# A long convolution with an MLP: three of K's channel blocks transposed by DMA, table G built from its non-zero parts

## The chip, the core and the metric

The kernel runs on one NeuronCore of a Trainium2 chip. The core has TensorE (PE, matmuls; PEld is its weight load), VectorE (DVE), ScalarE (ACT), GpSimd (POOL) and SyncE (SP), which here only issues transfers. Each engine works through its own list in order; they wait for each other by semaphores. SBUF is the on-chip memory of 128 partitions, PSUM the eight banks that TensorE writes and that ACT or DVE must empty ("evict") into SBUF. Sixteen DMA engines move data for all queues.

The metric is the device time of one execution in microseconds (us). The median of three runs before the change is 221.71 us (221.61 to 222.79).

## What is computed

```python
def reference(A_q, A_k, A_v, A_shift_k, A_ssm_k, A_ssm_D, B_x, B_w1, B_b1, B_w2):
    def _A_ref(q, k, v, shift_k, ssm_k, ssm_D):
        ...
        k_pad = jnp.pad(k, ((0, 0), (ks - 1, 0), (0, 0)))
        for t in range(ks):
            k_shift = k_shift + k_pad[:, t:t + S, :] * shift_k[:, ks - 1 - t][None, None, :]
        kv = k_shift * v
        ...
        y_f = kv_f * kf_f[None, :, :, :]
        y = irfft2(y_f)[:, 0, :S, :]
        y = y + kv * ssm_D[None, None, :]
        return q * y
    ...
    x = A_q
    h = x + _A_ref(_layernorm(x, axis=-1), A_k, A_v, A_shift_k, A_ssm_k, A_ssm_D)
    h2 = h + _B_ref(_layernorm(h, axis=-1), B_w1, B_b1, B_w2)
    return h2
```

(The two FFT calls are shortened in this listing.) There are 2048 positions and 640 channels, all bf16; the shift filter has four taps, the long filter ssm_k has 2048, and the MLP `_B_ref` is 640 to 1728 to 640 with the activation h * tanh(softplus(h)).

## The kernel before

**The algorithm.** The long causal convolution is a Fourier transform written as matmuls. The 640 channels are five blocks of 128 (dc, b or m = 0 to 4), grouped in three chunks: blocks 0 and 1, blocks 2 and 3, block 4. A transform has two stages: stage 1 (s1) is a matmul with cosine and sine tables over 128 positions, stage 2 (s2) one small matmul for each of 128 frequencies with a 128 x 128 matrix from table G. This is done for the filter (k in names: s1k, s2k) and for the product kv (v in names: s1v, s2v). Then the two spectra are multiplied (p1, p2; for p2 the filter's spectrum is needed with its partitions swapped in pairs, which the DMAs sw provide), and an inverse in two stages (i1, i2) gives y. Layernorms, the gate by q, and the MLP in two matmuls (m1, m2) follow.

**From raw K to kv.** K is loaded with positions on the partitions, in four parts (d_k0 to d_k3, line 525) into `ra`. For each block and each half h of a row's 16 positions, 8 transposes on TensorE (ktpe, line 590) bring the channels onto the partitions; the result, 1024 bf16 columns in one PSUM bank, is evicted by ACT or DVE (ktev, line 593, by the helper at lines 426 to 430) into `kt_s`. A third copy, shifted by one column, is made by GpSimd (ktsh, line 601). The shift filter is then a matmul (kspe, lines 609 and 610) with small banded matrices `wsh`, built by GpSimd (line 516); the eviction multiplies by V (kv, line 613, DVE).

**Table G.** It is a 128 x 16384 table (4 MB) that holds, for each frequency, a 128 x 128 matrix which is block-diagonal over four interleaved channels, so three quarters of it are zeros. It is loaded in eight pieces (d_g0 to d_g7, line 541), each as far as possible with long rows, and read as weights with step 1 (`g_v`, line 366) at lines 662 (s2k, 128 matmuls of 160 columns) and 697 (s2v, 128 of 64 and 128 of 96 columns).

**The order.** Every piece of work is an operation with a name, a cost and its dependencies; the list ORDER (lines 26 to 97) says in which order they go and, after the colon, on which engine: t TensorE, a ACT, v DVE, p GpSimd, d SP's DMA queue, s ACT's DMA queue. `_schedule` (line 181) walks the list and sets a start time for each from its cost and dependencies, and the operations are emitted by these times. So each engine's own order is that of the list. The names of the halves end in x and y. In the list before, SP's order is: the filter's five blocks d_n, x0, all of K, then pieces of G and the two halves of V (d_v1 early, d_v0 after four pieces of G), then the swaps sw0_1, sw0_0, sw2_0, sw0_3, sw0_2, sw1_0, d_a12, sw1_1, sw2_1, then the inverse's table and the weights of the MLP. GpSimd builds wsh, makes the shifted copies and takes nine of the sixteen products p1/p2 of chunk 0.

Of the kernel before, what the change touches and what calls it, by code (L numbers as in the profile page):

```python
# [12 lines left out]
BF16 = mybir.dt.bfloat16  # L13
# [3 lines left out]
S = 2048  # L17
D = 640
FF = 1728
FP = 1792  # L20
P = 128
# [5 lines left out]
d_id:s wz:v d_dr:s d_sk:s d_go:d wm:t d_n0:d d_n2:d d_n3:d d_x0:d d_n1:d d_n4:d d_k2:d dcpe:t warm:a dcev:v dq0:v k1pe0y:t k1pe0x:t k1pe2y:t d_k3:d  # L27
k1ev0y:v d_k1:d dq2:v k1pe2x:t k1ev0x:v k1ev2y:v k1ev2x:a s1kpe0_0x:t s1kev0_0x:v d_k0:d s1kpe0_3x:t s1kpe0_1y:t s1kpe0_2x:t s1kpe0_2y:t s1kpe2_2x:t
s1kpe2_3x:t s1kpe2_0y:t s1kev0_3x:a ln1_2:v s1kev0_2y:a s1kev0_2x:a dq1:v cfpe:t kz:p ln1p2:p s1kev2_3x:a dq3:v s1kev2_2x:a ln1_3:v s1kev0_1y:v dq4:v
d_g4:d k1pe3y:t k1ev3y:a coef:a d_v1:d wsh4_0:p ln1p3:p k1pe1x:t d_g3:d d_g2:d k1ev1x:a wsh2_1:p wsh0_0:p wsh4_1:p wsh1_1:p wsh3_1:p wsh2_0:p d_g1:d  # L30
k1pe1y:t k1pe3x:t k1ev1y:v k1pe4y:t k1pe4x:t k1ev3x:v k1ev4x:v s1kpe1_0y:t s1kpe2_2y:t s1kpe1_1y:t wsh1_0:p s1kev2_2y:a s1kpe2_1y:t k1ev4y:v
s1kpe3_0x:t s1kev1_0y:a s1kev2_0y:a s1kpe2_1x:t s1kpe1_1x:t s1kpe0_3y:t s1kev0_3y:a s1kev3_0x:v s1kev1_1x:v s1kpe4_0x:t s1kev4_0x:v s1kpe4_3y:t
s1kev4_3y:a s1kpe4_3x:t s1kpe2_0x:t s1kev2_1x:a s1kpe3_2y:t s1kpe4_2x:t ln1_0:v s1kev4_3x:v s1kev3_2y:v s1kev2_1y:a s1kpe0_1x:t s1kpe2_3y:t
s1kev1_1y:v ktpe2y:t s1kev4_2x:a ktev2y:v ktpe1y:t ktpe3y:t ktpe4y:t ktpe0x:t ktpe4x:t ktev1y:a ln1_1:v d_v0:d ktpe0y:t ktev3y:a s1kev2_0x:v ktev4x:v
ktev4y:v s1kev2_3y:a s1kev0_1x:a ktev0y:a ktpe3x:t ktpe2x:t s1kpe3_3y:t s1kpe3_2x:t s1kev3_3y:v s1kpe4_0y:t s1kpe4_1y:t s1kpe4_1x:t s1kev4_1y:a
s1kev3_2x:a s1kpe3_3x:t s1kpe1_3y:t ktev0x:v s1kpe0_0y:t ktev3x:v kspe3_1y:t s1kpe1_0x:t ktev2x:a s1kev1_3y:a s1kev4_0y:a ktpe1x:t s1kpe3_1y:t d_g0:d
s1kev1_0x:a s1kev0_0y:a s1kev3_1y:a s1kpe3_1x:t ktsh4:p wsh0_1:p s1kev4_1x:v ktsh1:p wsh3_0:p ktsh2:p ktsh0:p ln1p1:p ktsh3:p s1kev3_3x:v kv3_1y:v
s1kpe4_2y:t s1kpe1_2y:t ktev1x:v s1kev4_2y:a s1kev3_1x:v s1kpe1_2x:t d_small:p s1kpe3_0y:t s1kev1_2y:v s1kpe1_3x:t kspe0_1x:t kspe1_1x:t s1kev3_0y:v
s1kev1_2x:a s1kev1_3x:a s2kpe_9y:t s2kev_9y:a s2kpe_6x:t s2kev_6x:a s2kpe_5x:t s2kpe_3x:t s2kpe_10y:t kv0_1x:v s2kev_10y:a kv1_1x:v s2kpe_7y:t d_g6:d
d_g7:d d_g5:d s2kev_5x:v s2kpe_10x:t s2kev_3x:a kspe0_1y:t s2kpe_3y:t s2kev_3y:a s2kev_7y:v s2kpe_4x:t kspe0_0x:t s2kpe_6y:t kv0_1y:v kv0_0x:v  # L40
kspe0_0y:t s2kev_4x:a s2kev_6y:a kspe1_0x:t s2kpe_4y:t s2kev_10x:a kv0_0y:v s2kpe_8y:t s2kpe_7x:t s2kpe_8x:t s2kpe_2x:t kspe1_0y:t s2kev_4y:a
s2kpe_9x:t s2kev_7x:a kv1_0x:v s2kev_8x:a kspe1_1y:t s2kpe_5y:t s2kev_8y:v s1vpe0_2x:t kv1_0y:v s1vpe0_1x:t kv1_1y:v s1vev0_1x:v s1vpe0_1y:t
s1vpe0_0y:t s2kev_9x:a ln1p0:p s1vpe1_0x:t s1vpe1_0y:t s1vev0_0y:v s2kev_2x:a s2kev_5y:a s1vev0_2x:v s1vev0_1y:a s1vpe0_0x:t s1vpe1_2x:t s1vpe1_3y:t
s1vev1_3y:v s1vev1_2x:v s1vev1_0y:a s1vpe0_3x:t s1vpe1_2y:t s1vev1_0x:a s1vpe1_1x:t s1vev1_1x:v s1vpe0_2y:t s1vpe1_3x:t s1vev0_0x:v s1vev0_3x:a
s1vpe0_3y:t s1vpe1_1y:t s1vev1_2y:a s2kpe_15y:t kspe2_1x:t s1vev0_2y:a s1vev1_3x:a s1vev0_3y:a kv2_1x:v s2kpe_1x:t s2kpe_1y:t kspe4_0x:t kspe3_1x:t
s2kpe_20y:t s1vev1_1y:a s2vpe0_0x:t s2kev_1x:a s2kpe_0y:t kspe3_0x:t kv4_0x:v kv3_1x:v s2kev_1y:a kspe3_0y:t s2vpe0_4x:t s2kev_0y:a s2kev_20y:a
s2vpe0_3x:t s2vpe0_3y:t s2vev0_4x:a s2vev0_0x:v kv3_0y:v s2kev_15y:v s2vev0_3y:a kspe2_0y:t s2kpe_20x:t s2vev0_3x:a s2kpe_2y:t kspe4_1y:t s2vpe0_2x:t
s2kev_20x:a s2kev_2y:a kv3_0x:v s2kpe_17y:t s2kpe_14x:t s2vpe0_0y:t sw0_1:d s2vpe0_2y:t kv2_0y:v s2vev0_2x:v s2vev0_0y:v s2kev_17y:a s2kev_14x:a
kspe4_0y:t s2kpe_0x:t kspe2_1y:t s1vpe3_0x:t s2vev0_2y:a s2kev_0x:a kv4_0y:v kv4_1y:v s1vpe3_0y:t s1vev3_0y:a s2kpe_18x:t kspe2_0x:t s2kpe_19x:t
s2kpe_21:t p2_0_3:p p1_0_3:p s2kev_18x:a s1vev3_0x:a s2vpe0_6x:t kv2_0x:v s2kpe_16y:t s2kev_16y:a s2kpe_14y:t s2vpe0_1x:t s2vev0_1x:a s2kev_21:v  # L50
# [945 lines left out]
```

## Time and profile before

| what | us |
|---|---|
| median of three runs (lowest, highest) | 221.71 (221.61, 222.79) |
| profiled execution: span, first to last instruction | 219.6 |
| the same execution's whole time | not listed; runs' median less span: 2.1 |
| TensorE busy | 212.6 |
| weight loads busy | 157.8 |
| DVE busy | 145.1 |
| ACT busy | 133.1 |
| GpSimd busy | 75.6 |

The granted TensorE clock was 1.000 throughout. The page has six parts: busy time by engine; the span in 40 slices of about 5.5 us, each digit the busy share in tenths; the DMA queues; the chain of work that ended last; the costliest groups of instructions; and the DMA issues. In a group's row, `out<-in` are the names of tiles, then follow partitions x elements, the count, busy time, mean length of one in ns, and after the second bar the idle time of the engine just before, with what ended it. Busy time of TensorE includes the latency of a pipelined matmul, so two matmuls that overlap have lengths above their distance. The distance of two starts is what counts for throughput: in the rows of a timeline, that is the length of a group less the length of one, divided by the count less one.

### The profile page before, as it was taken

The numbers are of one execution on the slowest core, as the hardware profiler recorded it, in microseconds if no ns is written. First come the engines' busy times: TensorE is split into PE (matmuls) and PEld (weight loads), VectorE is DVE, ScalarE is ACT, GpSimd is POOL, SyncE is SP. The second block draws the span as 40 slices with busy tenths as digits, with TensorE's granted clock in tenths as the row PEclk, the third lists the DMA queues.
The fourth block names the chain that finished last, engine by engine and source line by source line (L and its number), as shares of the span: only waits on it lengthen the run. The fifth ranks groups of instructions, "written<-read, shape, count | busy, mean of one in ns | idle before, by whom it ended". The sixth has DMA issues, their size and how long they took to land.

```text
span 219.6 us, 6285 instructions
## 1 busy us (share of the span) xinstructions
PE 212.6 (97%) x2611; PEld 157.8 (72%) x2618; DVE 145.1 (66%) x324; ACT 133.1 (61%) x265; POOL 75.6 (34%) x112
## 2 busy tenths in 40 slices
PE   8999999999989999999999999999999999999993
PEld 2899889999879999899876644566554444656672
DVE  0799999999999999989699889883210000213023
ACT  2488899999999999997881178600036475300000
POOL 0079997089844007124883371411000000000000
PEclk9999999999999999999999999999999999999999
DMA  6999993417999906996004401552720000000113
GB/s 213 375 419 414 412 403 130 98 23 174 192 263 285 380 10 217 325 359 105 0 0 64 91 14 45 50 103 60 86 79 19 0 3 0 0 0 3 54 60 125
DMA packets 32876, 31.03 MB, mean 141 GB/s; under 512 B 19024, under 2 KB 29264, under 8 KB 32464
## 3 DMA queue, kind: packets, MB, share of 16 engines
q1 hardware_dynamic: 32384, 30.43, 46.3%
q8 instruction: 20, 0.33, 0.7%
q10 hardware_dynamic: 368, 0.20, 0.4%
q14 instruction: 8, 0.07, 0.1%
q0 software_dynamic: 96, 0.00, 0.0%
HBM read 20.47 MB, written 2.62 MB: 105 GB/s over the span
## 4 chain that ended last, share of the span: by engine, by line
PE 76%; ACT 11%; DVE 5%; issue 3%; SPq 2%; DMA 1%; DVEq 0%; ACTq 0%
PE ps L943 26%; PE ps L910 26%; ACT uk L428 8%; PE ps L813 4%; ACT uv L428 3%; PE ps L756 3%; PE ps L757 3%; PE ps L635 2%; PE ps L561 2%; PE ps L473 2%; PE ps L590 2%; DMA xa<-uk 1%; DVE ra L613 1%; PE ps L931 1%; DVE uv L716 1%
## 5 line engine op out<-in xcount | busy, mean ns | idle before, releaser
L910 PE MATMUL ps<-G 128*128 128x512 bf16 (+1 forms) x319 | 58.5, 336 | 0.3
L943 PE MATMUL ps<-rn,uv 128*128 128x320 bf16 (+2 forms) x415 | 58.5, 299 | 0.1
L915 ACT ACTIVATE uv<-ps,b1s 128x512 bf16<-128x512 f32 (+1 forms) x65 | 35.6, 607 | 36.6 <-PE ps L910 34.8
L943 PEld LDWEIGHTS <-uv 128*128 128x128 bf16 x416 | 39.2, 98 | 18.5 <-issue 1.6
L910 PEld LDWEIGHTS <-G 128*128 128x128 bf16 x325 | 31.1, 98 | 24.0 <-issue 0.9
L428 ACT CAST uk<-ps 128x512 bf16<-128x512 f32 (+1 forms) x91 | 47.2, 703 | 1.9 <-PE ps L562 1.4
L948 DVE TENSOR_TENSOR xb<-ps,xb 128x320 bf16<-128x320 f32 (+2 forms) x12 | 5.6, 488 | 42.6 <-ACT uv L915 24.3
L428 ACT CAST uv<-ps 128x512 bf16<-128x512 f32 (+2 forms) x54 | 28.6, 766 | 0.0
L430 DVE CAST uk<-ps 128x512 bf16<-128x512 f32 (+2 forms) x32 | 20.1, 661 | 0.6 <-ACT uk L428 0.5
L756 PE MATMUL ps<-a,uv 128*128 128x128 bf16 x160 | 18.7, 219 | 0.4 <-DVE uv L716 0.3
L756 PEld LDWEIGHTS <-uv 128*128 128x128 bf16 x160 | 17.8, 114 | 0.9 <-DVE uv L716 0.5
L837 POOL TENSOR_TENSOR r<-ve,mhalf 128x1 f32<-128x1 f32 x16 | 9.7, 613 | 25.0 <-DVE ve L834 24.9
L430 DVE CAST uv<-ps 128x512 bf16<-128x512 f32 (+2 forms) x28 | 17.2, 669 | 0.2 <-ACT uv L428 0.2
L948 DVE TENSOR_TENSOR xa<-ps,xa 128x320 bf16<-128x320 f32 x12 | 5.6, 486 | 14.0 <-PE ps L943 13.9
L613 DVE TENSOR_TENSOR ra<-ps,rb 128x512 bf16<-128x512 f32 x20 | 12.9, 683 | 0.3 <-ACT uv L428 0.3
L720 POOL TENSOR_TENSOR rn<-rn,uv 128x1024 bf16<-128x1024 bf16 x5 | 10.6, 2127 | 7.2 <-PE ps L697 7.2
L697 PE MATMUL ps<-uv,G 128*128 128x64 bf16 (+1 forms) x256 | 12.2, 197 | 0.8 <-ACT uv L428 0.6
L662 PE MATMUL ps<-uk,G 128*128 128x160 bf16 x128 | 12.4, 230 | 0.3 <-ACT uk L428 0.2
L697 PEld LDWEIGHTS <-G 128*128 128x128 bf16 x256 | 10.8, 96 | 1.4 <-issue 1.0
L428 ACT CAST rb<-ps 128x512 bf16<-128x512 f32 (+1 forms) x30 | 11.3, 464 | 0.7 <-PE ps L813 0.4
L561 PE MATMUL ps<-cst,ra 128*64 128x128 bf16 x160 | 10.7, 219 | 0.4
L562 PE MATMUL ps<-cst,ra 128*64 128x128 bf16 x160 | 10.9, 222 | 0.0
(111 smaller groups left out, 375.7 us busy)
## 6 DMA issues: line engine op xcount, KB each, us to landing
G<-tab_g SPq DMA_DIRECT2D x8, 512.0 KB, 14.1
rn<-in_A_ssm_k_dram SPq DMA_DIRECT2D x5, 512.0 KB, 6.3
ra<-in_A_k_dram SPq DMA_DIRECT2D x4, 640.0 KB, 11.4
rb<-in_A_v_dram SPq DMA_DIRECT2D x2, 1280.0 KB, 13.9
G<-in_B_w_dram SPq DMA_DIRECT2D x5, 432.0 KB, 7.3
rn<-in_B_w_dram SPq DMA_DIRECT2D x1, 2080.0 KB, 13.4
rn<-uk SPq DMA_DIRECT2D x8, 256.0 KB, 4.3
rb<-uk SPq DMA_DIRECT2D x8, 256.0 KB, 4.5
```

The source lines that it names most:

```text
L428: nc.scalar.copy(o, i)
L430: nc.vector.tensor_copy(o, i)
L561: nc.tensor.matmul(ps[0:64, k, :], lhs, mc, start=True, stop=True)
L562: nc.tensor.matmul(ps[64:128, k, :], lhs, ms, start=True, stop=True)
L613: nc.vector.tensor_tensor(kv_w[:, m, k:32:2, 8 * h:8 * h + 8, :], ps.rearrange("p (l t d) -> p d t l", l=4, t=8), raw_v[:, 8 * h:8 * h + 8 ...
L662: nc.tensor.matmul(ps[:, o:o + 160], g_v[:, f, :], KA[:, :, f, :], start=True, stop=True)
L697: nc.tensor.matmul(ps[:, fl * n:fl * n + n], g_v[:, f0 + h * kf + fl, :], VX[x][:, :, f0 + h * kf + fl, :], start=True, stop=True)
L756: nc.tensor.matmul(pz[:, k, :], V[c.i][:, dg // 4, :, dg % 4], a12[:, 0, :], start=True, stop=False)
L910: nc.tensor.matmul(ph[:, 0:w], w1[:, dc, fc * P:fc * P + P], lnhT_of(u)[:, dc, 0:w], start=(dc == 0), stop=(dc == NDC - 1))
L915: nc.scalar.activation(hb_of(u)[:, fc, 0:w], rt.tile[:, 0:w], ACT.Mish, bias=b1s[:, fc:fc + 1], scale=1.0)
L943: nc.tensor.matmul(po[:, 0:d1 - d0], hb_of(u)[:, fc, tl * P:(tl + 1) * P], w2[:, fc, d0:d1], start=False, stop=(fc == NFC - 2))
L948: nc.vector.tensor_tensor(x, rt.tile[:, 0:d1 - d0], x, ALU.add)
```

## The change

Three things change, and with them the whole order list.

1. Of K's five blocks, only 0 and 1 are still transposed by TensorE. For blocks 2, 3 and 4 (`KX`) an operation kp copies the 1024 raw columns of a block's half into a packed buffer KP (in the list all six by GpSimd), and a DMA transpose kx on SP's queue writes them to `kt_s`. KP lies in parts of `xb`, `hc` and `rn` that are free at that time; two of the kp wait for the filter's transposes (k1pe2), whose source lies there.
2. `kt_s` now holds the two halves next to each other, 272 columns per group, so that the shifted operand is a slice that begins one column earlier (15:143) instead of a copy: the five ktsh are gone. Column 15 is set to zero by kz.
3. Table G in DRAM has only the non-zero quarter, 1 MB. Four memsets (gz0 to gz3; gz1 on DVE, the others on GpSimd) clear the tile, and eight DMAs write the parts, each to every fourth partition in runs of 128 elements. In the tile, four frequencies are now interleaved, so a matmul's weights are read with step 4. A matmul of stage 2 waits for all four DMAs of its half of the table. The table a12 is permuted to match.

In the new list SP's order is: the filter's blocks, x0, d_g1, d_k1, d_g4, d_g0, d_k0, d_k2, d_g2, d_g6, d_g7, d_g5, d_g3, d_k3, d_v0, d_v1, then kx3_0, kx3_1, kx2_0, kx2_1, kx4_0, sw0_1, kx4_1, sw0_0, sw0_3, sw0_2, d_a12, sw1_0, sw1_1, sw2_1, sw2_0. GpSimd's is: gz0, gz2, gz3, six wsh, kz, ln1p3, ln1p2, kp2_0, kp3_0, a wsh, kp4_0, kp2_1, kp3_1, kp4_1, wsh2_1, ln1p0, wsh4_1, wsh3_1, ln1p1, d_small, then seven products of chunk 0 (nine before). On TensorE stage 1 of the filter comes first as a whole, then the first two ktpe, then stage 2 of the filter mixed with the rest; kspe3_0x is the first matmul that uses a DMA transpose. Counted by engine, ACT has 27, 23, 33, 13 and 21 of the evictions s1k, s1v, s2k, s2v of chunk 0 and s2v of the others (25, 24, 32, 11 and 19 before), DVE has the rest.

```diff
 ORDER = """
...
-    T["g"] = np.moveaxis(G, 4, 6).reshape(128, 128 * 128)
+    full = np.moveaxis(G, 4, 6).transpose(5, 0, 1, 2, 3, 4, 6)
+    T["g"] = np.stack([full[d, :, :, d].reshape(32, 32, 4, 32).swapaxes(2, 3).reshape(32, 128 * 32) for d in range(4)])
...
-    g_v = gt[:].rearrange("p (f q) -> p f q", q=P)
+    g_v = gt[:].rearrange("p (b q f) -> p b f q", q=P, f=4)
...
-    kt_s = [t[:, 0:3072].rearrange("p (g a t) -> p g a t", g=8, a=3) for t in at_uv]
+    kt_s = [t[:, 0:2176].rearrange("p (g n) -> p g n", n=272) for t in at_uv]
+    KX = [2, 3, 4]
+    KP = dict(zip([(m, h) for h in (1, 0) for m in KX], [xb[:, 0:1024], xb[:, 1024:2048], xb[:, 2048:3072], hc_t[:, 0:1024], *(rn[:, 4096 + 1024 * i:5120 + 1024 * i] for i in range(6))]))
...
-        return lambda: nc.sync.dma_start(gt[:, i * 2048:(i + 1) * 2048], dram["g"][:, i * 2048:(i + 1) * 2048])
+        d, h = i % 4, i // 4
+        return lambda: nc.sync.dma_start(gt[d:P:4, h * 8192:h * 8192 + 8192].rearrange("p (b q) -> p b q", q=512)[:, :, 128 * d:128 * d + 128], dram["g"][d, :, h * 2048:h * 2048 + 2048].rearrange("p (b q) -> p b q", q=128))
+    c_gz = [OP(f"gz{i}", [("dve", 1.77), ("pool", 3.5)], emit=(lambda e, i=i: (nc.vector if e == "dve" else nc.gpsimd).memset(gt[:, i * 4096:(i + 1) * 4096], 0.0))) for i in range(4)]
...
-        def shf(e, t=kt_s[b]):
-            nc.gpsimd.tensor_copy(t[:, :, 2, 1:128], t[:, :, 1, 0:127])
...
+        for h in (1, 0):
+            def kpf(e, b=b, h=h):
+                src = raw_k[:, h * 8 * D:(h + 1) * 8 * D].rearrange("p (n k r) -> p k r n", k=2, r=20)[:, :, 4 * b:4 * b + 4, :]
+                o = KP[b, h].rearrange("p (k r n) -> p k r n", k=2, r=4)
...
+            def kxf(e, b=b, h=h):
+                nc.sync.dma_start_transpose(kt_s[b][:, :, 144 - 128 * h:272 - 128 * h], KP[b, h])
...
-                    nc.tensor.matmul(o, t[:, q, h, :], w[:, 0:128], start=True, stop=False)
-                    nc.tensor.matmul(o[:, 0:48], t[:, q, 0 if h else 2, :], w[:, 128:176], start=False, stop=True)
+                    nc.tensor.matmul(o, t[:, q, 144 - 128 * h:272 - 128 * h], w[:, 0:128], start=True, stop=False)
+                    nc.tensor.matmul(o[:, 0:48], t[:, q, 144:272] if h else t[:, q, 15:143], w[:, 128:176], start=False, stop=True)
...
-    d_g = [DMA(f"d_g{i}", 0.525e6, emit_g(i), deps=d_n[:1], prio=0.6, lat=4.9) for i in range(8)]
+    d_g = [DMA(f"d_g{i}", 0.35e6, emit_g(i), deps=d_n[:1] + c_gz[i // 4 * 2:i // 4 * 2 + 2], prio=0.6, lat=4.5) for i in range(8)]
...
-                nc.tensor.matmul(ps[:, o:o + 160], g_v[:, f, :], KA[:, :, f, :], start=True, stop=True)
+                nc.tensor.matmul(ps[:, o:o + 160], g_v[:, f // 4, f % 4, :], KA[:, :, f, :], start=True, stop=True)
...
-                    nc.tensor.matmul(ps[:, fl * n:fl * n + n], g_v[:, f0 + h * kf + fl, :], VX[x][:, :, f0 + h * kf + fl, :], start=True, stop=True)
+                    nc.tensor.matmul(ps[:, fl * n:fl * n + n], g_v[:, (f0 + h * kf + fl) // 4, (f0 + h * kf + fl) % 4, :], VX[x][:, :, f0 + h * kf + fl, :], start=True, stop=True)
...
```

More of the change, by code (lines that the diff above doesn't have):

```diff
@@ L174 @@
 _MARK, _BLOCK, _FETCH = 199, 253, [(8, 4.7), (32, 6.2), (45, 3.0), (76, 5.5), (1e9, 4.2)]
-_PORT_DVE = r"(p[12]_|wsh|dadd|wb|h\d)"
-_PORT_POOL = r"(p[12]_|wsh|lnx|ktsh|dadd)"
+_PORT_DVE = r"(p[12]_|wsh|kp|dadd|wb|h\d)"
+_PORT_POOL = r"(p[12]_|wsh|lnx|kp|dadd)"
 _HOP = 0.04
@@ L363 @@
     rb = big.tile([P, NT * D], BF16, name="rb")
-    rn = big.tile([P, NT * D + 1024], BF16, name="rn")
-    g_v = gt[:].rearrange("p (f q) -> p f q", q=P)
+    rn = big.tile([P, NT * D], BF16, name="rn")
+    g_v = gt[:].rearrange("p (b q f) -> p b f q", q=P, f=4)
     w1 = gt[:, 0:NDC * FP].rearrange("p (c f) -> p c f", c=NDC)
@@ L648 @@
         s1_out[c.i] += make_s1("s1v", c, 0, b, [kv_ops[b]] * 4, 13.0 + 0.4 * c.i)
+    for i, k in enumerate(list(KP)[4:2 * len(KX)]):
+        [o for o in ops if o.name == f"kp{k[0]}_{k[1]}"][0].deps += k1_by[2 + i // 2]
     s1v_pes = [o for o in ops if o.name.startswith("s1vpe")]
```

180 lines of the change are left out of this document (93 added, 87 removed).

## The prediction

> **What bounds the kernel now.** I read the page first, then the chain of waits, then the waits and timelines of each engine up to 90 us. A timeline row gives start, length, engine, line, operation, count and the idle time before it.
>
> ```profile
> span 219.6 us, 6285 instructions
> PE 212.6 (97%) x2611; PEld 157.8 (72%) x2618; DVE 145.1 (66%) x324; ACT 133.1 (61%) x265; POOL 75.6 (34%) x112
> DVE  0799999999999999989699889883210000213023
> ACT  2488899999999999997881178600036475300000
> ```
>
> TensorE is busy to 97%, but a busy matmul row counts its latency too, so the second part of the page says more: up to slice 16 (88 us) ACT and DVE are full as well. The chain of waits splits the run in two.
>
> ```profile
> 18.42 4.60 PE ps L590 x72
> ...
> 87.09 2.92 PE ps L813 x28
> ...
> 204.88 11.44 PE ps L943 x91
> ```
>
> From 87.09 us on the chain is matmuls without a gap worth naming to 204.88 + 11.44 = 216.3: 129.2 us of inverse transform and MLP that the change does not touch. Before that it runs through evictions of PSUM by ACT and DVE. So whatever the change is worth must show as an earlier start of L813. ACT is the fuller of the two: these are all its waits between 8 and 90 us, and five stretches of its timeline.
>
> ```profile
> ACT rb L428 <- PE ps L635: 5.2, 1, 5.2
> ACT uk L428 <- PE ps L562: 1.4, 2, 0.7
> ACT uv L428 <- PE ps L590: 0.7, 1, 0.7
> ACT uk L428 <- PE ps L662: 0.5, 1, 0.5
> ```
>
> ```profile
> 8.31 1.01 ACT L428 COPY rb<-ps 128x1024 bf16<-128x1024 bf16 x1 [5.20 <-PE ps L635]
> 19.60 1.93 ACT L428 COPY uv<-ps 128x1024 bf16<-128x1024 bf16 x2 [0.74 <-PE ps L590]
> 30.48 6.58 ACT L428 CAST uk<-ps 128x480 bf16<-128x480 f32 x14 [0.50 <-PE ps L662]
> 54.37 15.05 ACT L428 CAST uv<-ps 128x512 bf16<-128x512 f32 x31
> 72.01 15.92 ACT L428 CAST uk<-ps 128x512 bf16<-128x512 f32 x32
> ```
>
> ```profile
> 80.00:87.10 7.10, 7.10 (x126) 1.00 0.39 128
> ```
>
> ACT's first eviction starts at 8.31 us (the 5.2 us lie before it) and its last of the inverse's first half ends at 72.01 + 15.92 = 87.93 us. Of these 79.6 us it waited 1.4 (twice 0.7) + 0.7 + 0.5 = 2.6; 77.0 are work. In a row, a bank of 512 fp32 costs it 15.05 / 31 = 0.485 us and a K tile of 1024 bf16 0.92 us (1.93 less 1.01). From 72 us on it drains 0.4975 us a bank, against 8 matmuls of 7.10 / 126 = 0.056 us (0.45; the window row: stretch, length, TensorE busy, matmuls, clock, DMA share, GB/s) that fill one: there ACT, not the array, sets the pace until DVE has finished its products.
>
> **The change part by part.** DVE's prices from its timeline, in a row:
>
> ```profile
> 6.09 0.17 DVE L488 COPY d_col<-ps 128x5 f32<-128x5 f32 x1 [5.16 <-PE ps L486]
> 24.12 1.28 DVE L430 COPY uv<-ps 128x1024 bf16<-128x1024 bf16 x2
> 36.37 4.28 DVE L430 CAST uv<-ps 128x512 bf16<-128x512 f32 x7
> 81.11 1.88 DVE L716 TENSOR_TENSOR uv<-uv,uk 128x1024 bf16<-128x1024 bf16 x3
> ```
>
> All three come to 0.60 us each (for example (4.28 - 0.68) / 6, with 0.68 the length of one).
>
> *Evictions.* Six K evictions go (ktev of blocks 2 to 4): three of ACT's four and three of DVE's six. The order list, counted name by name, also gives ACT six spectrum evictions (s1kev, s2kev, s2vev, net) that DVE had, and DVE two products p1/p2 that POOL had. ACT: -3 x 0.92 + 6 x 0.485 = **+0.15 us**. DVE: -3 x 0.60 - 6 x 0.60 + 2 x 0.60 = **-4.2 us**. So the fullest engine is not relieved at all; the sum of 3 x 0.92 + 3 x 0.60 = 4.6 us that vanishes from the two goes to DVE.
>
> *Transposes on TensorE.* 48 of 80 go. At 4.60 / 72 = 0.064 us that is 3.1 us of the array. It lies in a stretch (18.4 to 23.0) in which ACT waited 0.74 us for these transposes themselves and then 0.65 us for a stage-1 matmul queued behind them; the 0.50 us at 30.5 is the start of stage 2 of the filter, which waits until all of stage 1 has been drained. In the new order the two remaining K tiles of that stage come last, so ACT is fed by stage 1 without a break. I count these 1.9 us of waits as recovered. The other 0.74 us (13.9 to 14.85, the filter's own transposes ahead of stage 1) stays.
>
> *Weights of table G.* A stationary operand is now read with step 4, in 384 matmuls (L662, L697).
>
> ```profile
> L635 PEld LDWEIGHTS <-rn x80: 140/148/174, 6.0 to 13.9; 128*128 128x128 bf16 x80
> L697 PEld LDWEIGHTS <-G x256: 95/96/100, 41.4 to 70.4; 128*128 128x128 bf16 x128
> L756 PEld LDWEIGHTS <-uv x160: 111/113/118, 66.7 to 86.8; 128*128 128x128 bf16 x160
> ...
> 11.00 3.24 PE L635 MATMUL ps<-cst,rn 128*128 128x128 bf16 x48
> 42.64 0.86 PE L697 MATMUL ps<-uv,G 128*128 128x64 bf16 x24
> ```
>
> L756 already loads weights at step 4: 113 ns against 96. L635, at step 16, takes 148 ns and its matmuls follow each other at (3.24 - 0.23) / 47 = 64 ns, 84 less than the load. Less 84, a load at step 4 occupies 29 ns, which is just what the 64-wide matmuls need now: (0.86 - 0.19) / 23 = 29 ns. Bounds: nothing, or the 56 ns at which L756's 128-wide matmuls run, which are long enough to hide any load below that. I take 3 ns each for the 256 of L697, 0.8 us of an array that has just been given 3.1 us; L662's 160-wide ones are longer and pay nothing. The Trainium skill says in "TensorE: Matmul & The Clock Gate", section "Weight-path perf modes", that a fast weight load covers strided columns as well; by that the cost is nothing, the low end. The same page's plain load, columns over 1.2 GHz, would be about 107 ns and is ruled out by L756's pitch.
>
> *POOL: memsets, permutes, fewer copies.*
>
> ```profile
> L720 POOL TENSOR_TENSOR rn<-rn,uv 128x1024 bf16<-128x1024 bf16 x5 | 10.6, 2127 | 7.2 <-PE ps L697 7.2
> L516 POOL TENSOR_TENSOR uv<-cst,coef 128x704 bf16<-128x704 bf16 x5 | 6.8, 1366 | 0.8 <-ACT coef L428 0.8
> L601 POOL COPY uv<-uv 128x1016 bf16<-128x1016 bf16 x5 | 5.1, 1029 | 0.0
> L492 POOL MEMSET b1b<- 14x128 bf16 x1 | 0.2, 194 | 0.0
> L530 POOL MEMSET uv<- 128x8 bf16 x5 | 0.3, 135 | 0.0
> ...
> 11.24 0.23 POOL L791 TENSOR_SCALAR ve<-mv 128x1 f32<-128x1 f32 x1 [10.20 <-DVE mv L787]
> 12.23 0.26 POOL L793 TENSOR_SCALAR nmr<-mv,r 128x1 f32<-128x1 f32 x1
> ```
>
> Five copies of 1.03 us (ktsh) and two products of 2.13 go. Three memsets of 4096 elements come, at the start. Not shown at this size: from 8 to 128 elements a memset grows by 59 ns, 0.49 ns an element, so 2.1 us is the low end; the copy's 1.01 ns an element, which reads as well, gives 4.1 as the high end. I take 3.1, the middle, as neither row is nearer. The fourth (gz1) is DVE's, in the 5.16 us in which it waits anyway; without that cover it would cost its length. Six permutes (kp) of 1024 elements at a read step of 40: between the copy (1.03) and the two-input product (2.13); I take 1.5, nearer the copy, which has one input too.
>
> *SP and the DMA engines.* Six DMA transposes (kx) of eight 128-column tiles join SP's queue, between the loads of V and the swaps sw.
>
> ```profile
> L849 SPq DMA_TRANSPOSE G<-hc x14: 1200/1211/2649, 98.3 to 156.5; - x14
> ...
> DMA to landing us min/median/max: 2.6/2.7/4.1
> ...
> 60.00:65.00 5.00, 1.00 0.94 253
> ...
> GB/s 213 375 419 414 412 403 130 98 23 174 192 263 285 380 10 217 325 359 105 0 0 64 91 14 45 50 103 60 86 79 19 0 3 0 0 0 3 54 60 125
> ...
> G<-tab_g SPq DMA_DIRECT2D x8, 512.0 KB, 14.1
> 37.09 0.65 SPq L678 DMA_DIRECT2D rn<-uk  x1
> 47.63 0.59 SPq L678 DMA_DIRECT2D rn<-uk  x1
> ```
>
> Five tiles cost SP 1.21 us and land in 2.7; eight, scaled, 1.9 and 4.3: six are 11.6 us of SP, which issues nothing but one pair of swaps between 37.09 and 47.63. Only kx4_1 stands behind a swap (sw0_1), and its user kspe4 comes last. The swaps themselves stay behind the same evictions (s2kev of groups 13 and 14, late both times). G shrinks from 4 MB to 1 MB in runs of 256 B: at the 253 GB/s of the swaps, whose runs are as short, 4.1 us instead of 10.1 at the 415 of the page's first slices. No engine waited for a load of K, V or G before, so this buys nothing by itself; it pays for the new wait of SP: d_g4 stands behind the third memset, and behind d_g4 stand two of K's loads at once and, further on, the rest of K, G and V. The memsets end near 0.9 + 3 x 3.1 = 10.2 us; ahead of d_g4 4.0 MB are queued by their shapes (five filter blocks of 512 KB, x0 and one quarter of K of 640, one G of 128), 9.8 us of transfers at that rate. So the wait costs nothing at 3.1.
>
> *The sum.* ACT's last eviction of the inverse: 8.31 + 77.0 + 0.15 + 0.74 = 86.2 us instead of 87.93, **1.7 us** earlier, and the 129 us behind follow unchanged. The page gives the span of the profiled execution, 219.6 us, and not its whole time; the median of the runs, 221.71, lies 2.1 us above that span, which I leave as it is. 219.6 - 1.7 = 217.9 of span, **220.0 us** of time.
>
> **The rivals.**
>
> *The waits form again (221.9).* Same work on ACT, so if evictions of V or the start of stage 2 leave it 2.6 us of holes again, only the +0.15 is left. For it: ACT's list was packed without a hole from 31 us on, and there are new producers upstream. Against: DVE has 4.2 us of slack now to catch up.
>
> *K comes late (223.9).* The place is kspe3_0x, first user of a DMA transpose; TensorE takes its list in order, and stage 1 of V (s1vpe0), then ACT, are queued behind it. Its tile needs, on POOL in this order, three memsets (m each), six wsh (1.34), kz (0.4), two ln1p (1.25 each, 11.24 to 12.49 above), five permutes (c each), one more wsh, then 4.3 us to land: 0.9 + 3m + 8.0 + 0.4 + 2.5 + 5c + 1.3 + 4.3 = 17.4 + 3m + 5c = 34.2 us. It is wanted after ACT's stage 1 (27 x 0.485, four COPYs of 0.92 and coef, 0.5: 17.3 us from 8.3 on) and 27 evictions of stage 2 at 6.58 / 14 = 0.47, which makes 38.3, less some four banks in flight: about 36.5. So it decides from 3m + 5c = 19.1 on, against my 16.8. At both high ends it is 23.0: 3.9 us late, 221.7 - 1.7 + 3.9 = 223.9. The Trainium skill's "GPSIMD Engine Reference", section "Performance pitfalls for Q7 kernels", speaks for it: reads with a byte step over 8 take about 2.9 cycles an element instead of 1.9; that would be c = 2.5 us, an estimate, and 2.7 us late. The trace's unit-step copy runs at 1.2 cycles an element, below that page's 1.9, so the page's absolute figure is in doubt, not its ratio (c = 1.55).
>
> *Strided weights bind (223.1).* At the 56 ns bound a bank of V's first chunk takes 0.446 us of the array against 0.268 that ACT and DVE need together (0.485 and 0.60 in parallel): 16 x 0.178 + 26 x 0.01 = 3.1 us on top of 220.0. Against it: the 113 ns.
>
> **How the numbers follow.** Forecast 0.50 (own range 219.2, with no waits left, to 221.0), waits again 0.15, K late 0.22, weights 0.13. Runs of this kernel tell 0.5% (1.1 us) from no change: faster is below 220.6, slower above 222.8. Faster: 0.47 of the forecast's 0.50. Slower: 0.16 of K late, 0.12 of the weights, 0.02 of the waits, 0.30. Same: the remaining 0.23. The range, 218.9 to 224.2, takes in every case's own time; what is left out is a K chain later than both ends give, and a gain above the waits that exist.
>
> **What would show it.** Right: L813 starts near 85.4 us and what follows lasts 129 us; ACT waits under 1 us after its first eviction; L697's load at 113 ns with its 64-wide matmuls at 29 to 32 ns; kspe3 not released by a DMA. Wrong: ACT holes between 35 and 60 us ended by L561 behind a transpose (K late); POOL memsets over 4.1 us or permutes over 2.1; L697 at 40 ns or more; or a change behind L813, where I expect none.

## The result: 1% slower, and the profile after

The changed kernel took 224.39 us in the median of nine runs (222.58 to 227.47) against 221.71 before; the ratio is 1.010, with a 95% interval of 1.0074 to 1.0126. The forecast was 220.0 us and a range up to 224.2, so both the sign and the range were missed. The profiled execution was the shortest of the nine, 222.58 us with a span of 220.8, so the trace shows the smaller part of the loss: 1.2 us of span. In every execution on record the time is 1.7 to 1.9 us above the span, so the profiled execution of before, with 219.6 us of span, took about 221.4 us (an estimate) and is a short one too. The ratios leave out executions more than 1.5% above the shortest of the same kernel, among them one of the nine here, three of six with unit-step reads, and one of 429.42 us with the table part alone.

First the page of the changed kernel, the busy time of the engines and the slices (40 of 5.5 us each):

```profile
span 220.8 us, 6228 instructions
PE 211.8 (96%) x2570; PEld 157.4 (71%) x2570; DVE 144.1 (65%) x319; ACT 130.7 (59%) x265; POOL 91.6 (41%) x116
...
DVE  3469999999999999998999999861121000111141
ACT  2079999999999999998780347540301557200000
...
PEclk9879999999999999999999999999999999999999
```

Beside the page of before, the difference stands at the left edge: ACT does nothing in the second slice (4 tenths before), and TensorE's clock is not full in the second and third. From slice 4 on ACT is full. The chain of waits (the first three rows) begins with a load that the chain of before does not contain, and the start of the DVE, ACT and PE timelines says why (start, length, engine, line, operation, count, idle time before it):

```profile
1.30 1.76 DVE G L546
3.13 5.50 DMA sk_r<-in_A_shift_k_dram
8.68 0.88 PE ps L505 x9
...
3.01 0.06 DVE L466 MEMSET warm<- 128x2 f32 x1
...
3.12 0.20 ACT L467 ACTIVATE warm<-warm 128x2 f32<-128x2 f32 x1 [0.22 <-DVE warm L466]
3.13 0.33 ACTq L484 DMA_DIRECT2D sk_r<-in_A_shift_k_dram  x1
11.39 0.59 ACT L431 CAST uk<-ps 128x512 bf16<-128x512 f32 x1 [8.07 <-PE ps L567]
...
8.68 0.88 PE L505 MATMUL ps<-sk_r,cst 16*128 16x160 bf16 x9 [1.34 <-DMA sk_r<-in_A_shift_k_dram]
```

Read it downwards. On DVE the memset gz1 (L546) stands ahead of the 0.06 us memset of `warm`; ACT's warm-up activation waits for that one; and the load of `sk_r` is issued by ACT's queue behind the activation, at 3.13 us. (The row of before is shown with the first experiments: 1.68.) It lands 5.5 us later, and the new list has put cfpe, its reader, ahead of stage 1 of the filter on TensorE. So TensorE stops for 1.34 us, and then it runs at half its clock (windows of 1 us: stretch, length, TensorE busy, matmuls, clock, DMA share, GB/s):

```profile
8.00:9.00 1.00, 0.33 (x5) 1.00 0.96 367
9.00:10.00 1.00, 1.00 (x15) 0.93 1.04 417
10.00:11.00 1.00, 1.00 (x18) 0.50 0.98 401
...
12.00:13.00 1.00, 1.00 (x24) 0.50 1.01 356
13.00:14.00 1.00, 1.00 (x20) 0.87 1.06 349
```

ACT's first eviction comes at 11.39 us instead of 8.31. After that ACT hardly waits; the rest of its timeline up to the end of the inverse's first half:

```profile
15.13 1.01 ACT L431 COPY xa<-ps 128x1024 bf16<-128x1024 bf16 x1 [0.76 <-PE ps L650]
62.86 9.20 ACT L431 CAST uv<-ps 128x480 bf16<-128x480 f32 x20 [0.19 <-PE ps L714]
72.71 16.47 ACT L431 CAST uk<-ps 128x512 bf16<-128x512 f32 x33
```

The last eviction of that part ends at 72.71 + 16.47 = 89.18 us, 1.25 later than before (87.93): 3.08 of later start, less 1.65 of waits (0.95 instead of 2.6), less 0.2 of work (76.8 instead of 77.0). What follows lasts 220.8 - 89.18 = 131.6 us; before it was 219.6 - 87.93 = 131.7. So nothing happens behind that point, and each run below is read by three numbers of the same kind: ACT's first eviction, its idle time from there to the last eviction of the inverse's first half (waits of 0.15 us or more), and where that eviction ends.

| kernel | first eviction | ACT idle | last eviction | span | median of runs | ratio to before (95%) |
|---|---|---|---|---|---|---|
| before | 8.31 | 2.6 | 87.93 | 219.6 | 221.71 | |
| after | 11.39 | 0.95 | 89.18 | 220.8 | 224.39 | 1.010 (1.0074 to 1.0126) |
| after, repeated | 11.11 | 1.6 | 90.16 | 221.8 | 223.42 | 1.0086 (1.0058 to 1.0114) |
| warm-up first | 9.09 | 2.8 | 89.16 | 220.8 | 223.49 | 1.0085 (1.0058 to 1.0112) |
| cfpe later | 8.59 | 6.0 | 92.41 | 224.2 | 224.37 | 1.0087 (1.0048 to 1.0126) |
| both cures of the start | 8.98 | 4.8 | 91.53 | 223.3 | 224.01 | 1.0084 (1.0055 to 1.0113) |
| kp3_1 up only | 11.62 | 0.6 | 89.10 | 220.8 | 223.16 | 1.0067 (1.0034 to 1.010) |
| warm-up first, kp3_1 up | 8.74 | 1.6 | 87.80 | 219.4 | 221.23 | 0.998 (0.9956 to 1.0004) |
| warm-up first, short memsets | 9.31 | 3.4 | 90.19 | 221.9 | 222.79 | 1.0024 (0.9988 to 1.0059) |
| all three | 9.58 | 0.5 | 87.28 | 219.1 | 221.74 | 0.9992 (0.9959 to 1.0025) |
| all three, k1pe2y later | 9.13 | 2.0 | 88.81 | 220.8 | 222.34 | 1.0014 (0.9991 to 1.0038) |
| cfpe later, kp3_1 up | 8.75 | 2.0 | 88.36 | 220.0 | 221.85 | 0.9995 (0.9981 to 1.0008) |
| warm-up first, unit-step reads | 8.79 | 3.9 | 90.02 | 221.9 | 222.60 | 0.9958 (0.9919 to 0.9997) |
| the same, V behind two transposes | 9.31 | 4.9 | 91.99 | 223.5 | 225.44 | 1.0176 (1.0145 to 1.0207) |
| before, table part alone | 8.65 | 3.2 | 89.37 | 221.0 | 222.36 | 1.001 (0.9994 to 1.0026) |

In every row the span less the last eviction is 131.5 to 132.0 us, and last less first less idle is 76.8 to 77.9 us of work. First eviction, idle time, last eviction and span are of one profiled execution each. Each ratio is to executions of the kernel before that were taken together with it (medians 221.46 to 221.86 us), so ratios compare better than medians do. The profiled execution of "cfpe later", 225.96 us, is the longest of its seven.

### The profile page after: what moved, and what is told of

It is laid out like the page before. It is cut to its first block, busy times and chain, and to the rows that moved or that the text cites. A ratio compares the mean times of both kernels' runs of the same rounds, so it can differ in the third digit from the quotient of the medians.

```text
span 220.8 us, 6228 instructions
## 1 busy us (share of the span) xinstructions
PE 211.8 (96%) x2570; PEld 157.4 (71%) x2570; DVE 144.1 (65%) x319; ACT 130.7 (59%) x265; POOL 91.6 (41%) x116
## 4 chain that ended last, share of the span: by engine, by line
PE 65%; DVE 19%; ACT 6%; DMA 4%; issue 3%; POOL 1%; ACTq 0%; DVEq 0%
PE ps L960 19%; PE ps L927 19%; PE ps L679 4%; PE ps L774 4%; PE ps L773 4%; DVE st L803 4%; PE ps L566 4%; DVE st L849 3%; ACT uv L431 3%; ACT uk L431 3%; DMA sk_r<-in_A_shift_k_dram 2%; PE ps L714 2%; PE ps L624 2%; DVE rb L840 2%; PE ps L650 1%
## 5 line engine op out<-in xcount | busy, mean ns | idle before, releaser
L960 PE MATMUL ps<-rn,uv 128*128 128x320 bf16 (+2 forms) x416 | 57.9, 299 | 0.0
L433 DVE CAST uk<-ps 128x512 bf16<-128x512 f32 (+1 forms) x29 | 18.0, 668 | 1.0 <-ACT uk L431 0.5
L433 DVE CAST uv<-ps 128x512 bf16<-128x512 f32 (+1 forms) x25 | 15.4, 674 | 0.0
L519 POOL TENSOR_TENSOR uv<-cst,coef 128x704 bf16<-128x704 bf16 x10 | 13.5, 1371 | 1.4 <-ACT coef L431 1.4
L714 PE MATMUL ps<-uv,G 128*128 128x64 bf16 (+1 forms) x256 | 12.3, 202 | 1.6 <-DVE uv L433 1.2
L714 PEld LDWEIGHTS <-G 128*128 128x128 bf16 x256 | 11.3, 115 | 2.2 <-DVE uv L433 1.3
L679 PE MATMUL ps<-uk,G 128*128 128x160 bf16 x128 | 11.6, 232 | 0.1
L733 DVE TENSOR_TENSOR uv<-uv,uk 128x1024 bf16<-128x1024 bf16 (+1 forms) x15 | 11.0, 766 | 0.5 <-POOL rn L737 0.4
L431 ACT CAST rb<-ps 128x512 bf16<-128x512 f32 (+1 forms) x29 | 10.7, 463 | 0.9 <-PE ps L830 0.8
L830 PE MATMUL ps<-uk,ra 128*128 128x256 bf16 (+1 forms) x96 | 10.7, 255 | 0.0
```

The costliest lines, as they stand in the source:

```text
L431: nc.scalar.copy(o, i)
L433: nc.vector.tensor_copy(o, i)
L519: (nc.gpsimd if e == "pool" else nc.vector).tensor_tensor(out, a, b, ALU.mult)
L679: nc.tensor.matmul(ps[:, o:o + 160], g_v[:, f // 4, f % 4, :], KA[:, :, f, :], start=True, stop=True)
L714: nc.tensor.matmul(ps[:, fl * n:fl * n + n], g_v[:, (f0 + h * kf + fl) // 4, (f0 + h * kf + fl) % 4, :], VX[x][:, :, f0 + h * kf + fl, :], ...
L733: eng.tensor_tensor(v, v, K[c.i][:, b0:b1, f0:f1, :], ALU.mult)
```

## The experiments

### The start

**The change once more.**

> The changed kernel once more, for a second profile of it and its spread. Theory S (a late start: the load of sk_r is issued at 3.1 us instead of 1.7, because ACT's warm-up waits for a small memset that stands behind gz1 on DVE; cfpe waits for it on TensorE ahead of the filter's transposes, and the pause costs the clock): ACT's first eviction at about 11.4 us again, against 8.3 in the kernel before. Theory M (what is lost lies in the middle: DMA transposes, strided weights or permutes): the first eviction may move from run to run, but the time follows holes on TensorE or ACT between 30 and 70 us.

223.42 us (222.64 to 224.96). Its profiled execution starts as late (11.11) and idles somewhat more: the loss is no accident of one series.

**The warm-up's memset ahead of gz1.**

```diff
-        nc.vector.memset(warm[:], 0.0)
-    c_wz = OP("wz", ("dve", 0.95), emit=lambda e: nc.vector.memset(wz, 0.0), prio=-5)
+    c_wz = OP("wz", ("dve", 0.95), emit=lambda e: (nc.vector.memset(wz, 0.0), nc.vector.memset(warm[:], 0.0)), prio=-5)
```

> The changed kernel with the memset of warm issued right after wz, ahead of gz1. Theory S: sk_r issued at about 1.7 us and landed by 6.5, cfpe waits under 0.2 us, the clock stays at 1.00 in 10 to 15 us, ACT's first eviction at 8.4, L830 starts near 85.5 and the time is 220 to 221, about 1% under the kernel before. Theory M: the start is as early, but the time stays within 0.5 us of the changed kernel, above 223.

The start is cured (`sk_r` is issued at 1.68 us again, as in the kernel before) and the time is not: 223.49 us. Two rows of ACT's timeline, TensorE's longest wait between 8 and 90 us, and the window in which the time went (stretch and length, then the busy time of TensorE, weight loads, DVE, ACT and POOL, then clock, DMA share and GB/s):

```profile
9.09 0.58 ACT L431 CAST uk<-ps 128x512 bf16<-128x512 f32 x1 [5.98 <-PE ps L566]
40.80 0.56 ACT L431 CAST uk<-ps 128x480 bf16<-128x480 f32 x1 [1.95 <-PE ps L678]
...
PE ps L624 <- DMA uv<-xb: 2.2, 1, 2.2
...
35.00:40.00 5.00, 2.82 (x56) 2.66 (x54) 3.48 (x6) 3.85 (x9) 4.73 (x6) 1.00 1.12 126
```

L624 is kspe, and `uv<-xb` the DMA transpose that it waits for. TensorE works 2.82 of these 5 us (in the kernel after it works all 5) and then ACT stands still for 1.95. Of the 2.3 us won at the start this one wait takes back most, and the last eviction ends at 89.16 us, as in the kernel after (89.18). The row of the kernel before for `sk_r`:

```profile
1.68 0.46 ACTq L481 DMA_DIRECT2D sk_r<-in_A_shift_k_dram  x1
```

**cfpe later, and both cures.** In the order list cfpe goes from ahead of k1pe2y to behind s1kpe0_2y, and its eviction coef behind s1kev0_2y.

```diff
-... d_n3:d cfpe:t d_n4:d k1pe2y:t ... s1kev0_1x:a coef:a ...
+... d_n3:d d_n4:d k1pe2y:t ... s1kpe0_2y:t cfpe:t ... s1kev0_2y:a coef:a ...
```

> The changed kernel with cfpe moved behind seven stage-1 units on TensorE (and coef behind their evictions on ACT), sk_r still issued late. Theory S: TensorE and ACT no longer wait for sk_r, ACT's first eviction at about 8.4, the time 220 to 221.5 (wsh, which needs coef, starts at 12 to 13 as in the changed kernel). Theory M: above 223.

> Both edits. Theory S: no more than either alone, 220 to 221, since each removes the same wait. Theory M: above 223.

224.37 us (1.0087, 1.0048 to 1.0126) and 224.01. Again ACT starts in time (8.98 with both) and TensorE waits for K: 3.1 us with both, after which the clock is at 0.50 for three microseconds. That a late start alone explains the loss is refuted, by three kernels.

The wait at K has a second price. The record gives the mean granted clock of every execution, and one stretch of 3.4 us at 0.50 lowers a mean over 220 us to 0.992. With the warm-up first, eight of eleven executions lie at 0.984 to 0.992 and took 223.19 to 224.90 us; the three at 0.999 and 1.000 took 222.51 to 223.08. Both cures of the start show the same: 221.87 and 222.78 us at 1.000, ten executions of 223.62 to 225.59 at or below 0.992. The profiles of both cures and, below, of the short memsets show the clock fall right behind the wait at K. So the median there is that of executions which lost the wait and the clock. In the changed kernel itself the clock does not decide: its two executions at 1.000 took 223.77 and 224.01 us.

### K's transposes

**kp3_1 up, with and without the cured start.**

```diff
-kp3_0:p wsh1_0:p kp4_0:p ... kp2_1:p ... kp3_1:p kp4_1:p
+kp3_0:p wsh1_0:p kp3_1:p ... kp2_1:p ... kp4_0:p kp4_1:p
```

> The kernel after with ScalarE's warm-up memset right behind wz (as in the run with the warm-up first, 223.49 us), and with the permute of K's block 3, second half (kp3_1), moved on POOL ahead of kp4_0 and kp2_1, which stood ahead of it at 2.28 us each. Theory 'two gates in a row' (the late start hides K's late transposes; either alone is worth nothing): the transposes of block 3 are issued some 4.5 us earlier (about 30.2 instead of 34.68), PE's 2.2 us wait of kspe3 for the transpose goes, and with it the 2.0 us that ACT waited behind it: 221.3 us (220.6 to 222.0). Rival 'the loss lies in the new order of the evictions or of the second-stage work, not in K': no change from the warm-up first, 223.5 (222.9 to 224.1), and another wait takes the place.

> The kernel after with only kp3_1 moved ahead of kp4_0 and kp2_1 on POOL; the start stays late. Theory 'two gates in a row': PE comes to kspe3 after the transposes anyway, since it started 3 us late, so K's 4.5 us earlier are worth nothing: 224.0 us (223.4 to 224.6). Rival 'K's transposes alone set the time': 221.5 to 222.5.

221.23 us with the cured start, 223.16 without: the two gates stand one behind the other, and only opening both brings the time down. POOL's permutes, first with the warm-up first, then with kp3_1 up as well (and there two rows of ACT):

```profile
22.00 2.30 POOL L610 COPY hc<-ra 128x1024 bf16<-128x1024 bf16 x1
30.08 6.83 POOL L610 COPY xb<-ra 128x1024 bf16<-128x1024 bf16 x3
```

```profile
27.84 4.55 POOL L610 COPY xb<-ra 128x1024 bf16<-128x1024 bf16 x2
...
39.08 0.56 ACT L431 CAST uk<-ps 128x480 bf16<-128x480 f32 x1 [0.21 <-PE ps L678]
71.33 16.47 ACT L431 CAST uk<-ps 128x512 bf16<-128x512 f32 x33
```

A permute takes (6.83 - 2.30) / 2 = 2.27 us in a row. kp3_1, the second of the three, ended at 34.6 and now ends at 30.1 (the first of its two); ACT's wait at stage 2 shrinks from 1.95 to 0.21 us. With the late start the same edit is worth at most a little: its ratio of 1.0067 and those of the two runs of the change overlap, and its median lies 0.2 us under the range expected. The clock comes back too: with both edits nine of ten executions kept 0.999 or more and took 220.93 to 222.66 us, and the tenth, at 0.992, took 224.26.

**Short memsets.** The zeros of G written as 2048 words of 32 bits each, without and with kp3_1 up.

```diff
-.memset(gt[:, i * 4096:(i + 1) * 4096], 0.0)
+.memset(gt[:, i * 4096:(i + 1) * 4096].bitcast(F32), 0.0)
```

> The warm-up memset first, and the four memsets of table G written as 2048 32-bit zeros each instead of 4096 bf16 zeros; order unchanged. If POOL's memset goes by elements, each takes about 1.75 us instead of 3.47, everything on POOL behind them comes up to 5.2 us earlier, SP's d_g4 is released at about 6 instead of 11.16, and K is early by another way than by the order: 221.3 us (220.6 to 222.0), with PE's wait for the transpose gone. If it goes by bytes, 3.47 us stay and the time is that of the warm-up first, 223.5. Rival 'not K': POOL shorter but 223.5 all the same.

> Warm-up memset first, kp3_1 moved up, and G's zeros as 32-bit words, all three. Theory 'two gates in a row': with both gates open already by either cure, the third edit adds nothing measurable: 221.0 us (220.4 to 221.8), within 0.4 of the better of the two. Rival 'POOL binds at further places behind K' (its wsh and the p products): up to 1 us below the better of the two.

A miss that teaches something. POOL's timeline without kp3_1 up, then TensorE's wait for the transpose and windows of 1 us behind it:

```profile
0.72 5.29 POOL L545 MEMSET G<- 128x2048 f32 x3 [0.29 <-POOLq L996]
10.40 8.00 POOL L518 TENSOR_TENSOR uv<-cst,coef 128x704 bf16<-128x704 bf16 x6 [4.39 <-ACT coef L431]
...
21.24 2.31 POOL L610 COPY hc<-ra 128x1024 bf16<-128x1024 bf16 x1
29.33 6.81 POOL L610 COPY xb<-ra 128x1024 bf16<-128x1024 bf16 x3
...
39.17 0.20 PE L624 MATMUL ps<-uv 128*128 128x48 bf16 x1 [2.15 <-DMA uv<-xb]
...
40.00:41.00 1.00, 1.00 (x23) 0.61 1.22 252
41.00:42.00 1.00, 1.00 (x24) 0.50 0.55 101
42.00:43.00 1.00, 1.00 (x25) 0.50 0.00 0
```

A memset falls from 3.47 us (three take 10.41 in the kernel after) to 1.76, and POOL then waits 4.39 us for coef: the permutes begin at 21.24 instead of 22.00. The wsh ahead of the permutes need coef, so behind sk_r and cfpe the memsets were hidden but for 0.8 us, and POOL could not be shortened there; TensorE's wait for the transpose stays at 2.2 us in this execution (223.76 us), and the clock is at 0.50 behind it. The ratio, 1.0024, is lower than with the warm-up first (1.0085), but the intervals touch; four of the ten executions kept the full clock and took 220.73 to 222.57 us, and none of these was profiled. With kp3_1 up the shorter memsets add nothing that can be measured (0.9992 against 0.998), as expected.

**Permutes that read at unit step.**

```diff
-src = raw_k[:, h * 8 * D:(h + 1) * 8 * D].rearrange("p (n k r) -> p k r n", k=2, r=20)[:, :, 4 * b:4 * b + 4, :]
+src = raw_k[:, h * 8 * D + (b - 2) * 1024:h * 8 * D + (b - 1) * 1024].rearrange("p (k r n) -> p k r n", k=2, r=4)
```

> The warm-up memset first, order as in the changed kernel (223.49 us in that run), and the six permutes kp read 1024 neighbouring elements of K instead of a step of 40 elements (80 bytes), so K's blocks 2 to 4 hold other elements than the reference's. If the step of the read is what makes c 2.28 us, a permute falls to 1.0 to 1.3 us (the unit-step copy of before took 1.03), K's block 3 is transposed 5 to 6 us earlier, PE's 2.2 us wait for the transpose goes: 221.3 us (220.6 to 222.0). If the step costs nothing, c stays near 2.28 and the time at 223.5. Rival 'not K': c falls, 223.5 stays.

Six executions of 219.83 to 224.6 us, median 222.6; the ratio of 0.9958 (0.9919 to 0.9997) rests on three of them, so here it says less than the spread. The profiled one took 223.68, at full clock. POOL's and SP's timelines of it:

```profile
26.28 3.00 POOL L610 COPY xb<-ra 128x1024 bf16<-128x1024 bf16 x3
...
23.05 0.81 SPq L537 DMA_DIRECT2D rb<-in_A_v_dram  x2
24.05 5.63 SPq L615 DMA_TRANSPOSE uv<-rn  x1
29.78 6.02 SPq L615 DMA_TRANSPOSE uv<-xb  x1
```

The step of the read is indeed what a permute costs: 1.04 us instead of 2.28. kp3_1 ends at 28.3, six us earlier. Yet in this execution TensorE waits 2.0 us for kx3_1 (and 0.8 for kx3_0): SP takes 5.63 and 6.02 us to issue the first two, right behind V's loads.

**The same, with those two transposes ahead of V's loads.**

```diff
-... d_k3:d d_v0:d d_v1:d ... kp3_1:p ... kx3_0:d kx3_1:d ...
+... d_k3:d ... kp3_1:p kx3_0:d kx3_1:d d_v0:d d_v1:d ...
```

> As the run with unit-step reads (permutes of 1.04 us, K's blocks 2 to 4 hold other elements than the reference's), but SP issues the first two transposes (kx3_0, kx3_1) ahead of the two loads of V instead of behind them. In the run before, these two took SP 5.63 and 6.02 us to issue, from 24.05 to 35.8 us, while V's 2.56 MB were under way; a transpose takes 1.3 to 1.5 us where nothing is. Theory 'the transposes stand behind V's loads in the DMA queues': both are issued in under 1.6 us each, the second right after its permute (28.3), by 30 us, and PE's wait of 2.0 us for uv<-xb is gone; V is issued at about 30 instead of 23 and its readers on DVE (kv) wait for it, so the time is no better: 222 to 226. Rival 'a transpose is slow by itself when the permute that feeds it has just ended, or behind the last load of K and the table': 4 us or more again for at least one of the two.

```profile
24.07 1.34 SPq L615 DMA_TRANSPOSE uv<-rn  x1
28.35 1.23 SPq L615 DMA_TRANSPOSE uv<-xb  x1
29.69 2.02 SPq L537 DMA_DIRECT2D rb<-in_A_v_dram  x2
31.77 2.23 SPq L615 DMA_TRANSPOSE uv<-hc  x1
34.04 6.71 SPq L615 DMA_TRANSPOSE uv<-xb  x1
```

Ahead of V the transposes take 1.34 and 1.23 us, and the ones now behind V take 2.23 and 6.71: a transpose can be held up in issue while V's 2.56 MB are under way. How long differs from run to run: with the warm-up first and kp3_1 up, V is issued at 23.51, and the transposes at 26.58 and 30.16 took 1.47 and 2.88 us. As expected the time is no better (225.44 us of two executions), since now DVE waits 3.6 us for V. So K's chain has two parts, POOL's permutes and SP's queue behind V, and either can make it late.

### The other parts

**Before, with the part on table G alone.** The tables g and a12, the loads, the four memsets (gz1 ahead of `warm`) and the weights at step 4 as in the change; K and the order list as before, except that the gz stand in front and d_g5 to d_g7 behind d_g0.

> The kernel before with the part on table G alone: G loaded without zeros in runs of 256 B, three POOL memsets and one on DVE (ahead of the warm-up's memset, as in the changed kernel), weights read at step 4; K's path and the order list else as before. Theory: all of it is covered: d_sk is issued at 3.1 here too, but cfpe stands behind a dozen stage-1 matmuls in this order and finds sk_r landed; strided weights pay nothing: 221.8 us (221.2 to 222.5). Rival 'strided weights bind': up to 3 us more, 224 to 225, with the 64-wide matmuls over 32 ns apart. Rival 'the late warm-up hurts by itself': first eviction of ACT later than 8.4, 222.8 to 224.5.

222.36 us, ratio 1.001 (0.9994 to 1.0026): within what can be told from no change. Strided weights do not bind (24 matmuls of 64 columns take 0.96 us here too, 0.86 before), and gz1 ahead of `warm` does not hurt where cfpe stands behind stage 1: the first eviction is at 8.65.

**The other cure of the start, with kp3_1 up.** The edits of "cfpe later" and "kp3_1 up" together.

> The other cure of the start with the cure of K: cfpe later (as in that run, 224.37 us, where PE waited 2.9 us for K's transpose), the warm-up memset left behind gz1, kp3_1 moved up by two permutes (4.5 us). Theory 'two gates in a row': any cure of the start goes with any cure of K: the 2.9 us wait is gone, 221.4 us (220.7 to 222.2). Rival 'only the warm-up cures the start': 223.0 or more.

221.85 us, ratio 0.9995: cures of the two gates can be exchanged.

**A version that was to beat both.** All three edits, and k1pe2y moved behind s1kpe0_1x.

```diff
-... cfpe:t d_n4:d k1pe2y:t ... s1kpe0_3x:t s1kpe0_1x:t k1ev2y:v
+... cfpe:t d_n4:d ... s1kpe0_3x:t s1kpe0_1x:t k1pe2y:t k1ev2y:v
```

> A version meant to have both gates open and the start as early as before: warm-up memset behind wz, kp3_1 moved up, G's zeros as 32-bit words (as in the run with all three, whose ACT waited only 0.5 us between its first eviction at 9.58 and the end of the inverse's first half), and k1pe2y (0.72 us of TensorE) moved from ahead of the first stage-1 matmuls to behind s1kpe0_1x. Theory (ACT's ledger: start + 77.2 us of work + waits): the first eviction comes 0.5 to 0.7 us earlier than in the runs without it (8.74 and 9.58), the time is 220.5 us (219.8 to 221.2), a ratio near 0.995. Rival: the tile of k1pe2y is then late for stage 1 and a wait of ACT gives it back: 221.2, ratio 0.998.

222.34 us, ratio 1.0014: slower than theory and rival had it. The first eviction comes at 9.13, 0.45 us earlier than with the three edits alone. ACT then waits 0.82 us for a tile of the filter's transposes, as the rival said, but it is one of block 1 (`xa`) and not the moved one (`rb`, which DVE evicts); how the move delays it is not shown. Another 0.86 us of waits fall between 61 and 64 us, where the clock of this execution falls to 0.50. No version that reads K as the reference does beats the kernel before beyond its interval; warm-up first with kp3_1 up, 0.998, is the best of the design.

## Why the prediction was wrong

**The step that failed first: gz1 "in the 5.16 us in which it waits anyway".** For DVE's own work that was right. What I did not list is who waits behind it: the memset of `warm`, then ACT's activation, then an issue on ACT's queue, then the load of sk_r, then cfpe, which the new list puts in front. The prediction took the start as unchanged at 8.31; it was 11.39. In the ten kernels of the change with a cured start it was 8.59 to 9.58. Why 0.3 to 1.3 us stay is open. One part is visible: ACT's first eviction was a tile of the filter's transposes before (`rb`) and is the first bank of stage 1 now (`uk`), which in seven of the ten has cfpe's 0.8 us of TensorE ahead of it. Moving k1pe2y away won 0.45 us and lost it again.

**The second: K comes late.** It was a rival, at 0.22 and 223.9 us, and it is what the kernel does once the start is cured: 2.2 us of TensorE, 223.49 us. That 223.49 lies so near 223.9 is luck: the rival had 3.9 us of wait and no loss at the clock. I put it below the forecast because of c = 1.5, "nearer the copy", for the permute; it measured 2.28, above my high bound of 2.13. The Trainium skill, "GPSIMD Engine Reference", section "Performance pitfalls for Q7 kernels", gives about half again as much for a byte step over 8, and the estimate from it was 2.5. The runs agree with the direction and show a larger ratio, 2.28 / 1.04 = 2.2. I had named that page's rule and then priced it as a rival only because its absolute figures did not fit a unit-step copy. The memsets measured 3.47 against my 3.1, so 3m + 5c was 21.8 against 19.1, 2.7 us late by the prediction's own rule, and 2.2 were measured: the rule was right and its two terms were mis-sized. It lacked two things that other runs show: the wsh wait for coef as well as for the memsets, so a smaller m would have helped by 0.8 us at most, and the transposes stand behind V's loads on SP, whose time I had scaled from transposes with nothing ahead of them. With the warm-up first the six took 10.9 us of SP against the 11.6 I had, so the second mattered only where K was early.

**A term put at nothing: the clock.** The prediction has no row for a drop of the clock, as the kernel before had none (1.000). With the waits that it opened the clock dropped in most executions: seven of nine of the kernel after, eight of eleven with the warm-up first.

**Why the two were not added.** In the kernel after, the late start hides the late K: ACT's evictions begin 2.3 us later than with the warm-up first (11.39 against 9.09), and TensorE finds the transposes landed at kspe3. So its profile shows only the first gate, and a theory read from that profile alone fell with the first three kernels.

**Recovered waits.** 1.9 us were counted. In the four kernels with both gates open the idle time of ACT is 0.5 to 2.0 us against 2.6 before: 0.6 to 2.1 recovered. With kp3_1 up and the warm-up first it is 1.0, and the later start (0.43) and 0.4 us more of work take it back, and the last eviction ends at 87.80 against 87.93. So part of the forecast's mechanism was there, and the 1.7 us were not, even with both gates open. With short memsets as well it ended 0.65 us earlier (87.28), in one execution.

**What was right.** The work on ACT came to 76.8 to 77.9 us, forecast 77.15. What lies behind ACT's last eviction of the inverse's first half did not change (131.5 to 132.0 us in every run). L813's first matmul was the wrong mark for that: with both gates open it starts at 85.8 us, near the 85.4 named as a sign of being right, against 86.9 before, yet the span is only 0.2 us shorter. Two more of those signs came true in the slower kernel after, for another reason than the forecast's: ACT waited 0.95 us and kspe3 was not released by a DMA, both, as the cured starts show, because everything began late. Strided weights cost about what I took: in the view of line L714 and TensorE's timeline of the kernel after,

```profile
L714 PEld LDWEIGHTS <-G x256: 111/114/133, 45.8 to 69.0; 128*128 128x128 bf16 x128
...
45.89 0.96 PE L714 MATMUL ps<-uv,G 128*128 128x64 bf16 x24
```

the load takes 114 ns, as L756's did (113), and 24 matmuls take 0.96 us, 0.86 before: (0.96 - 0.19) / 23 = 33 ns apart instead of 29. I had added 3 ns; the run with the table part alone shows no longer time for it that could be told from none. SP's wait for the third memset (d_g4 at 11.16 us) cost nothing either: with the short memsets it was issued at 7.4 and no wait went away for it.

**What stays open.** DVE was to be relieved by 4.2 us; its busy time from 8 to 88 us fell from 78.1 us before to 76.3 with the warm-up first and kp3_1 up, and why not by more is open. The two profiled executions of the kernel after account for 1.2 and 2.2 us, where the medians differ by 2.7 and 1.9. No profile shows an execution of it above 223.58 us, or one at full clock; whether these lost their time at K, the second gate, or elsewhere is not known.

## What to carry to other kernels

Price a short instruction that is moved to the head of a queue by the whole line behind it: follow each waiter, onto the next engine and onto that engine's DMA queue, until something lands. When a change opens a wait early on, look for a second one that the first hides: take the first away in one kernel, and test each cure alone and both together before giving the loss a cause. A DMA transpose on a queue behind a large load is priced with that load, and a GpSimd copy with its read step.

## What the runs showed of the hardware

TensorE's clock fell to 0.50 for about 3.4 us after a pause of 1.34 us in the kernel after. After a pause of 2.2 us at kspe3 it stayed at 1.00 in one execution (warm-up first) and fell to 0.50 in another (short memsets): the length of a pause alone does not decide it. The Trainium skill, "TensorE: Matmul & The Clock Gate", section "The HAM clock gate (the "warmup" mystery)", ties the drop to an idle window of about 3.4 us whose place is free-running; the length of the half clock agrees, while here a pause well under one window was enough.

A POOL memset of 4096 bf16 took 3.47 us, the same bytes as 2048 words of 32 bits 1.76: here it went by elements. A copy of 1024 bf16 on POOL took 1.04 us at unit step and 2.28 at a step of 80 bytes. A DMA transpose of eight tiles took SP 1.23 and 1.34 us to issue ahead of V's loads, and up to 6.71 behind their 2.56 MB.
